# A pooled attention with a top-2 mixture of experts: whole-row gathers and scatters, spread over partition groups through scratch, late zeros and a moved drain

## The chip, the core and the metric

The kernel runs on one core of one Trainium2 chip. The metric is the device time of one execution in microseconds; lower is better. The core has five engines: PE (TensorE) multiplies matrices, DVE (VectorE) and ACT (ScalarE) work elementwise, POOL (GpSimd) works elementwise and issues the indirect DMAs, that is gathers and scatters whose row numbers come from a tile, and SP (SyncE) issues plain DMAs. Each engine carries out its instructions in order and waits for others by semaphores.

## The reference

Two parts follow each other. The attention has 8 batches, 8 heads, 576 tokens, head size 64; keys and values are first averaged over groups of 8 tokens, so each query meets 72 pooled rows. Its output, 4608 tokens of 512 numbers, goes through a noisy top-2 mixture of 8 experts (512 to 1024 to 512):

```python
k_p = k.reshape(B, H, Sp, pool, D).mean(axis=3)
v_p = v.reshape(B, H, Sp, pool, D).mean(axis=3)
attn = softmax(scale * np.matmul(q, k_p.transpose(0, 1, 3, 2)))
x = (attn @ v_p).transpose(0, 2, 1, 3).reshape(4608, 512)
noisy = x @ w_gate + np.log1p(np.exp(x @ w_noise)) * noise
# the two largest of 8 per token; their softmax weighs the two experts
for e in range(E):
    for k in range(2):
        mask = top2[:, k] == e
        h = np.maximum(x[mask] @ w1[e], 0.0)
        out[mask] += top2_w[mask, k, None] * (h @ w2[e])
```

(The softmax is written out in the reference; it is shortened here.) Each token is thus worked on by two experts, and its two contributions are added in its row of the output.

## The kernel before

**Attention.** Work goes in 4 pairs of batches, each cut into 9 chunks of 128 tokens, 36 chunks in all. Eight of the nine (kind "D") belong to one batch; the ninth (kind "R") holds the last 64 tokens of both. SP loads q, k and v. Keys and values are pooled by adding halves: the first addition of the values of batches 2 to 7 is on POOL (`halves`, L237, chosen by the bit mask PV = 252), the others on DVE (L243, L249). `pe_prep` multiplies the pooled values by a mask into block tiles `vbd` on POOL (L317, main part) and DVE (L332). `qk` (L371, L378) makes scores, `et` transposes their exponentials, `av` (L410) multiplies by `vbd`. A row multiply on DVE (L421) makes the chunk's x, kept as `lastx`, which SP or POOL writes to `x_dram` (L428, L431).

**Zeros.** The output is added to row by row, so it is first filled with zeros: `zero` (L124) is nine plain DMAs of 1 MB on SP, one in each of the chunks from 27 on. They stand under `issue_after(lastx[0].ins)`, which orders them in the program and makes SP wait for nothing.

**Routing.** `route` finds each token's two experts and weights and its place in each expert's list. For each 128 tokens and each of the two choices, POOL scatters 128 records of 8 bytes (token number, weight) into `rec_dram` (L593, 72 DMAs). `load_recs` (L621) reads the lists back and works out the index tiles. For expert 0 these hold token numbers. For the others `late()` and `spread()` work out, by small matmuls with a selection matrix (L634), a quarter-row index: each row of x is seen as four rows of 128 numbers, and each 32 tokens of a tile are spread so that every partition group of 32 holds a quarter of their row (`x4`, `out4`, `oi4`, `wc4`).

**Experts.** The list of an expert is cut into tiles of 128 tokens. Three groups follow each other: tiles 0 to 3, then the tail (tiles 7 to 9, at most 320 tokens, of which PE picks one of three widths, 320, 272 or 240, by the count), then tiles 4 to 6. For group i the program emits in this order: `stage1` of group i (first product, L943, by 8 blocks of 128 hidden units; ACT takes the ReLU into `hh`, L950; DVE takes the rest into `hl`, L951), `split` of group i+1, `fetch` of group i+2, `stage2` of group i. Every product is done in three passes of high and low parts in fp32r. The framework orders the instructions of each engine by priority and readiness.

`fetch` gathers rows of x on POOL. For expert 0 it is one indirect DMA per tile (L675). For the others it is four per tile (two for tile 9), each of 128 quarter rows (L683):

```python
for r in range(2 if t == 9 else 4):
    nc.gpsimd.indirect_dma_start(
        out=xg[:, r * P:(r + 1) * P], out_offset=None, in_=x4,
        in_offset=bass.IndirectOffsetOnAxis(ap=xi[e, t][:, r], axis=0))
```

There are four buffers `xg`. `split` transposes a tile, on PE for expert 0 (L871), else on DVE by 32 x 32 blocks (L877), and makes the high part on ACT and the low part on DVE (L882).

`stage2` of a group of full tiles takes each tile by itself: `prev` reads the present rows of the output (L963, one whole-row gather on POOL into one of three `pv` buffers), 24 matmuls (L1037), `finish` adds the weighted result on DVE in four parts (L978), and POOL scatters the rows back (L981). A first `prev` of an expert has to wait for the last scatter of the expert before. The tail's `stage2` makes the transposed product (L1008), transposes it back on DVE by 32 x 32 blocks into `yt` (L1015), and works by quarter rows: 10 gathers of the output (L995), 10 additions on DVE (L1021), 10 scatters (L1024).

**Weights.** `weights` loads 512 KB pieces on SP (L458, 64 of them) into three staging buffers `wst`; ACT makes the high part (L468) and DVE the low (L469).

After the last group comes a loop for tokens beyond the lists' capacity, which makes no trip with these inputs, and a closing barrier with drains of each engine (L1215).

## Time and profile before

| | |
|---|---|
| time, median of 3 runs | 1265.1 us (1261.36 to 1266.04) |
| profiled execution | 1265.68 us |
| its span in the profile | 1263.9 us |
| mean granted clock of TensorE | 0.903 |
| PE busy | 1082.7 us (86%), 5858 matmuls |
| DVE / ACT busy | 559.8 us (44%) / 343.7 us (27%) |
| POOL busy | 687.2 us (54%), 690 instructions |
| first matmul of the experts | at 263.0 us |
| last matmul | ends at 1248.1 us |

The span is what the profiler saw of one execution; the execution's time is 1.8 us longer. A granted clock of 1.00 is 2.4 GHz and 0.50 is 1.2 GHz; a mean between them is a mixture of both. "issue" as the releaser of an idle time means that the engine waited for nothing that the profile shows. Times in the rows are microseconds from the start of the span.

### The profile page before, as it was taken

The numbers are of one execution on the slowest core, as the hardware profiler recorded it, in microseconds if no ns is written. First come the engines' busy times: TensorE is split into PE (matmuls) and PEld (weight loads), VectorE is DVE, ScalarE is ACT, GpSimd is POOL, SyncE is SP. The second block draws the span as 40 slices with busy tenths as digits, with TensorE's granted clock in tenths as the row PEclk, the third lists the DMA queues.
The fourth block names the chain that finished last, engine by engine and source line by source line (L and its number), as shares of the span: only waits on it lengthen the run. The fifth ranks groups of instructions, "written<-read, shape, count | busy, mean of one in ns | idle before, by whom it ended". The sixth has DMA issues, their size and how long they took to land. (4 is left out here: it accounts for less than half of the span.)

```text
span 1263.9 us, 16358 instructions
## 1 busy us (share of the span) xinstructions
PE 1082.7 (86%) x5858; PEld 937.6 (74%) x5858; DVE 559.8 (44%) x1323; ACT 343.7 (27%) x862; POOL 687.2 (54%) x690
## 2 busy tenths in 40 slices
PE   7887698369899878979997899899989997898895
PEld 6876588258788578858885788588869885786794
DVE  5786557363236233614361436234513551361341
ACT  4675376140123012301230123013301330131110
POOL 3345553726547635773577357645764576566131
PEclk7999689679899788989898889799979998999897
DMA  9998795233115221522152215221622261222110
GB/s 265 311 303 175 188 283 189 56 117 86 44 42 176 69 67 51 188 69 62 51 175 76 63 52 184 66 72 51 196 56 71 50 196 53 74 52 74 52 32 27
DMA packets 78143, 141.05 MB, mean 112 GB/s; under 512 B 26391, under 2 KB 34604, under 8 KB 78036
## 3 DMA queue, kind: packets, MB, share of 16 engines
q1 hardware_dynamic: 49876, 76.88, 21.3%
q0 software_dynamic: 28160, 62.70, 16.9%
q8 instruction: 73, 1.20, 0.4%
q14 instruction: 34, 0.28, 0.1%
HBM read 102.27 MB, written 39.17 MB: 112 GB/s over the span
## 5 line engine op out<-in xcount | busy, mean ns | idle before, releaser
L943 PE MATMUL ph<-xh,w 128*128 128x384 f32 (+4 forms) x1536 | 417.6, 352 | 59.6 <-ACT xh L882 25.3
L683 POOL DMA_INDIRECT xg<-x_dram,x x266 | 283.5, 1066 | 143.6 <-issue 74.4
L943 PEld LDWEIGHTS ph<-xh,w 128*128 128x128 f32 x1536 | 286.9, 199 | 91.6 <-issue 35.6
L1037 PE MATMUL py<-w,hh 128*128 128x512 f32 x896 | 300.2, 412 | 25.1 <-issue 22.8
L943 PE MATMUL ph<-xl,w 128*128 128x512 f32 (+4 forms) x768 | 270.1, 352 | 4.2 <-issue 3.2
L950 ACT ACTIVATE hh<-ph 128x512 fp32r<-128x512 f32 (+2 forms) x192 | 97.0, 508 | 638.8 <-PE ph L943 204.2
L1037 PEld LDWEIGHTS py<-w,hh 128*128 128x128 f32 x896 | 176.7, 199 | 73.7 <-issue 39.0
L951 DVE SCALAR_TENSOR_TENSOR hl<-ph,hh 128x512 fp32r<-128x512 f32 (+2 forms) x192 | 109.2, 577 | 255.9 <-ACT hh L950 196.2
L1037 PE MATMUL py<-w,hl 128*128 128x512 f32 x448 | 185.2, 413 | 15.8 <-issue 15.3
L943 PEld LDWEIGHTS ph<-xl,w 128*128 128x128 f32 x768 | 152.5, 199 | 19.6 <-issue 5.8
L978 DVE SCALAR_TENSOR_TENSOR pv<-py,raw,pv 128x128 f32<-128x128 f32 x196 | 54.8, 343 | 242.2 <-remote 142.8
L1024 POOL DMA_INDIRECT out_dram<-pv,o x80 | 82.9, 1036 | 80.2 <-DVE pv L1021 53.0
L981 POOL DMA_INDIRECT out_dram<-pv,raw x56 | 57.5, 1027 | 123.6 <-DVE pv L978 108.3
L1037 PEld LDWEIGHTS py<-w,hl 128*128 128x128 f32 x448 | 88.8, 198 | 43.5 <-issue 26.5
L593 POOL DMA_INDIRECT rec_dram<-rec,pos x72 | 73.2, 1016 | 75.7 <-DVE cum L1122 23.8
L1008 PE MATMUL py<-hh,w 128*128 128x240 f32 (+2 forms) x512 | 99.8, 293 | 0.1
L469 DVE TENSOR_TENSOR w<-wst,w 128x512 fp32r<-128x512 f32 x128 | 82.9, 685 | 22.7 <-issue 9.6
L468 ACT CAST w<-wst 128x512 fp32r<-128x512 f32 x128 | 73.0, 618 | 70.3 <-DMA wst<-in_moe_w_dram 50.7
L1008 PEld LDWEIGHTS py<-hh,w 128*128 128x128 f32 x512 | 82.5, 192 | 0.8 <-issue 0.8
L995 POOL DMA_INDIRECT pv<-out_dram,o x70 | 71.4, 1020 | 21.3 <-issue 19.2
L385 ACT ACTIVATE ex<-s,mx 128x72 f32<-128x72 f32 x288 | 69.2, 340 | 30.9 <-DVE mx L383 29.9
L1008 PE MATMUL py<-hl,w 128*128 128x240 f32 (+2 forms) x256 | 74.9, 292 | 1.3 <-issue 1.3
(153 smaller groups left out, 1063.9 us busy)
## 6 DMA issues: line engine op xcount, KB each, us to landing
wst<-in_moe_w_dram SPq DMA_DIRECT2D x64, 512.0 KB
v<-in_v_dram SPq DMA_DIRECT2D x24, 448.0 KB
out_dram<-zt SPq DMA_DIRECT2D x9, 1024.0 KB
k<-in_k_dram SPq DMA_DIRECT2D x7, 1280.0 KB
q<-in_q_dram SPq DMA_DIRECT2D x7, 1024.0 KB
x_dram<-xr POOLq DMA_DIRECT2D x12, 512.0 KB
xg<-x_dram,x POOLq DMA_INDIRECT x276
x_dram<-xr SPq DMA_DIRECT2D x4, 512.0 KB
```

The costliest lines, as they stand in the source:

```text
L385: nc.scalar.activation(ex[:, jj, EPOS[h] * G:(EPOS[h] + 1) * G], sv[:, i], AF.Exp, bias=mx[:, i:i + 1])
L468: nc.scalar.copy(hv, sv)
L469: nc.vector.tensor_sub(lv, sv, hv.bitcast(F32))
L593: s = nc.gpsimd.indirect_dma_start(out=rec_dram[:, :], out_offset=bass.IndirectOffsetOnAxis(ap=pos[:, i, c:c + 1], axis=0), in_=rec[:, c, ...
L683: nc.gpsimd.indirect_dma_start(out=xg[:, r * P:(r + 1) * P], out_offset=None, in_=x4, in_offset=bass.IndirectOffsetOnAxis(ap=xi[e, t][:, r ...
L943: nc.tensor.matmul(part(ph), w1s(e, a, db, f), part(xs[b][:, db]), start=(i == 0), stop=(i == 3 * NDB - 1))
L950: nc.scalar.activation(hh[:, :n], ph[:, :n], AF.Relu)
L951: nc.vector.scalar_tensor_tensor(hl[:, :n], ph[:, :n], 0.0, hh[:, :n].bitcast(F32), op0=OP.max, op1=OP.subtract)
L995: g = nc.gpsimd.indirect_dma_start(out=pv4[:, i], out_offset=None, in_=out4, in_offset=bass.IndirectOffsetOnAxis(ap=oi4[e, t0 + i // 4][:, ...
L1008: nc.tensor.matmul(part(py), w2s(e, b, f)[:, mb * P:(mb + 1) * P], part(hs[f][a]), start=(i == 0), stop=(i == 3 * NFB - 1))
L1024: s = nc.gpsimd.indirect_dma_start(out=out4, out_offset=bass.IndirectOffsetOnAxis(ap=oi4[e, t0 + i // 4][:, i % 4], axis=0), in_=r4[:, i], ...
L1037: nc.tensor.matmul(py, hs[f][a][:, cs], w2s(e, b, f), start=(i == 0), stop=(i == 3 * NFB - 1))
```

## The change

- The quarter-row indices are taken out: `sel`, `qcol`, `late`, `spread` with its small matmuls, `oi4`, `wc4`, `x4`, `out4`, `pv4`. The index tile is worked out directly from the records, on POOL for expert 0 and on DVE for the others.
- `gather` of experts 1 to 7 becomes one whole-row indirect DMA per tile into `row` (two buffers), a plain DMA by SP of that tile into a DRAM scratch `via` (four buffers), and four plain DMAs by SP (two for tile 9) from there into the four quarters of `xg`.
- The tail reads the output by `prev`, whole rows of three tiles, so that it uses the three `pv` buffers too. Its transposed result goes from `yt` by ten plain DMAs of SP into a scratch `viay`, by three more into `ys`, and each of its three tiles is finished by one wide DVE instruction and one whole-row scatter.
- `zero` gets a real dependency: each of the nine DMAs waits for the row multiply (DVE) of its chunk.
- PV becomes 0: the values' halves are added on DVE. The main part of `vbd` (16 products) goes from POOL to DVE.
- In chunks of kind R, the scores of both row halves are emitted together, alternating, and the loops of `av` alternate the two token halves.
- In the last `stage1`, after its fourth block, POOL drains, ordered after the last scatter sent by then.

```diff
-    PK, PV = 0, 252
+    PK, PV = 0, 0
@@
-            nc.gpsimd.tensor_mul(vb[:BST, ss, :D].rearrange("p (n i) d -> p n i d", i=ns),
+            nc.vector.tensor_mul(vb[:BST, ss, :D].rearrange("p (n i) d -> p n i d", i=ns),
@@
+            if g == 0:
+                SR[u] = [ps2.tile([P, 512], F32, tag="s", name=f"s{nm}_{k}", bufs=SB) for k in range(2)]
+                for i in range(4):
+                    for b2 in range(2):
+                        for k in range(2):
+                            nc.tensor.matmul(SR[u][k][b2 * 64:b2 * 64 + 64, i * G:(i + 1) * G],
...
@@
-            for r in range(2 if t == 9 else 4):
-                nc.gpsimd.indirect_dma_start(
-                    out=xg[:, r * P:(r + 1) * P], out_offset=None, in_=x4,
-                    in_offset=bass.IndirectOffsetOnAxis(ap=xi[e, t][:, r], axis=0))
+            nr = 2 if t == 9 else 4
+            row = pools[0].tile([P, DM], F32, tag="row", name=f"row{e}_{t}", bufs=2)
+            nc.gpsimd.indirect_dma_start(
+                out=row[:32 * nr], out_offset=None, in_=x_dram[:, :],
+                in_offset=bass.IndirectOffsetOnAxis(ap=xi[e, t][:32 * nr], axis=0))
+            via = dp.tile([P, DM], F32, tag="via", name=f"via{e}_{t}", bufs=4)
+            nc.sync.dma_start(via[:32 * nr], row[:32 * nr])
+            for r in range(nr):
+                nc.sync.dma_start(xg[:, r * P:(r + 1) * P],
+                                  via[32 * r:32 * r + 32].rearrange("j (u c) -> u j c", u=4))
@@
-                with tc.issue_after(lastx[0].ins):
-                    zero((i - ZS) // ZD)
+                zd = zero((i - ZS) // ZD)
+                tc.add_manual_dep(zd.ins, lastx[0].ins.name,
+                                  mybir.DependencyInfo(mybir.DependencyClass.Sync, mybir.DependencyReason.DATA),
+                                  reason="paced by the chunks")
@@
+            pvs = [prev(e, t, P) for t in range(7, 10)]
...
+            for t in range(7, 10):
+                nr = 2 if t == 9 else 4
+                ys = mp.tile([P, DM], F32, tag="ys", name=f"ys{e}_{t}", bufs=2)
+                via = dp.tile([P, DM], F32, tag="viay", name=f"viay{e}_{t}", bufs=3)
+                for r in range(nr):
+                    nc.sync.dma_start(via[32 * r:32 * r + 32].rearrange("j (u c) -> u j c", u=4),
+                                      yt[:, 4 * (t - 7) + r].rearrange("p m c -> p (m c)"))
+                nc.sync.dma_start(ys[:32 * nr], via[:32 * nr])
+                finish(e, t, P, ys, pvs[t - 7], 32 * nr)
             return
@@
+    def flush(f):
+        if f == 3:
+            with tc.issue_after(sent[-1].ins):
+                nc.gpsimd.drain()
@@
-        stage1(g, (hook0, hook2)[i] if i < 2 else None)
+        stage1(g, hook0 if i == 0 else flush if i == len(groups) - 1 else None)
```

## Rows read from the trace of the kernel before

**Rows 1.** Busy time in stretches, one for each expert (experts 2 and 6 here, the longest and the shortest of experts 1 to 6). Columns: stretch, its length, busy time (and instructions) of PE, weight loads, DVE, ACT and POOL, mean granted clock, mean DMA share, GB/s.

```profile
515.20:642.30 127.10, 115.22 (x554) 99.04 (x553) 51.37 (x104) 27.12 (x52) 75.80 (x72) 0.92 0.31 92
...
1015.90:1136.50 120.60, 107.53 (x554) 91.50 (x553) 49.86 (x101) 24.75 (x48) 76.45 (x74) 0.94 0.28 84
```

**Rows 2.** The same view for the matmuls of one line alone, in stretches in which that line runs without a pause: the first product with 512 columns (L943), the second with 512 (L1037), the first with 384 (L943), the tail's second with 320 (L1008). Columns: stretch, length, busy PE (and matmuls), clock, DMA share, GB/s.

```profile
642.20:664.30 22.10, 21.92 (x96) 1.00 0.60 194
1231.60:1248.20 16.60, 16.52 (x72) 1.00 0.10 35
1216.30:1231.80 15.50, 15.44 (x88) 1.00 0.09 28
589.30:600.20 10.90, 10.72 (x72) 1.00 0.16 43
```

**Rows 3.** Stretches inside expert 2, columns as in rows 1.

```profile
556.00:571.30 15.30, 7.71 (x18) 3.92 (x17) 0.33 (x2) 0.00 (x0) 8.92 (x10) 0.67 0.23 69
571.30:605.90 34.60, 32.89 (x196) 31.11 (x195) 13.00 (x29) 5.15 (x11) 15.85 (x17) 0.95 0.21 65
605.90:611.20 5.30, 3.36 (x12) 2.21 (x11) 0.33 (x1) 0.49 (x1) 1.72 (x2) 0.79 0.14 37
611.20:642.30 31.10, 31.10 (x147) 28.25 (x146) 21.15 (x45) 11.02 (x21) 19.05 (x15) 0.93 0.30 82
```

**Rows 4.** The timeline of the weight loads between 556 and 571 us, two following ones. Columns: start, duration, engine, line, operation, count; in brackets the idle time before and its releaser.

```profile
556.89 0.19 PEld L1037 LDWEIGHTS py<-w,hh 128*128 128x128 f32 x1 [0.51 <-issue]
557.57 0.19 PEld L1037 LDWEIGHTS py<-w,hl 128*128 128x128 f32 x1 [0.50 <-issue]
```

**Rows 5.** The timeline of POOL in expert 2: the first and the last of the run of 27 indirect DMAs (3 of L963, 10 of L995, 8 of L683, one each of L981 and L963, 4 of L683), and the first and the last of the run of twelve of L683.

```profile
532.62 1.04 POOL L963 DMA_INDIRECT pv<-out_dram,raw  x1 [2.01 <-DMA out_dram<-pv,raw]
...
566.71 0.95 POOL L683 DMA_INDIRECT xg<-x_dram,x  x1 [0.30 <-issue]
...
593.13 0.98 POOL L683 DMA_INDIRECT xg<-x_dram,x  x1 [5.26 <-DVE xt L877]
...
606.98 0.95 POOL L683 DMA_INDIRECT xg<-x_dram,x  x1 [0.30 <-issue]
```

**Rows 6.** The same slow stretches in experts 1 and 3 to 6 (a short one of expert 1 stands second), columns as in rows 1.

```profile
423.00:438.00 15.00, 9.54 (x21) 4.68 (x20) 1.13 (x4) 0.00 (x0) 9.34 (x10) 0.67 0.15 38
479.50:486.00 6.50, 3.31 (x11) 2.27 (x10) 0.00 (x0) 0.06 (x1) 3.16 (x4) 0.74 0.15 42
681.00:699.30 18.30, 9.17 (x18) 4.13 (x16) 1.12 (x4) 0.00 (x0) 11.60 (x12) 0.58 0.24 68
802.50:815.70 13.20, 8.10 (x17) 3.48 (x15) 0.00 (x0) 0.00 (x0) 7.92 (x9) 0.67 0.17 42
926.40:939.00 12.60, 7.23 (x16) 3.88 (x16) 0.00 (x0) 0.00 (x0) 7.65 (x8) 0.63 0.16 42
1045.60:1063.30 17.70, 10.43 (x34) 5.92 (x33) 0.00 (x0) 0.00 (x0) 11.62 (x12) 0.89 0.15 39
```

**Rows 7.** Expert 0: the first and the last of a run of twelve on POOL's timeline, and the busy times of the stretch around it, columns as in rows 1.

```profile
315.52 0.97 POOL L683 DMA_INDIRECT xg<-x_dram,x  x1 [0.99 <-issue]
...
329.36 0.95 POOL L683 DMA_INDIRECT xg<-x_dram,x  x1 [0.30 <-issue]
...
315.50:333.00 17.50, 12.75 (x80) 12.37 (x79) 2.92 (x7) 1.70 (x5) 11.44 (x12) 0.79 0.20 56
```

**Rows 8.** PE's waits between 388.8 and 1248 us: the one for the split's copy by ACT, which lies in expert 7. Columns: engine and line, what was waited for, us in total, times, longest.

```profile
PE ph L943 <- ACT xh L882: 8.3, 1, 8.3
```

**Rows 9.** SP. Its waits over the whole span (for the copy that frees a staging buffer of weights, and for the plain write of a table that it reads back next), and the issue of the weight loads and of the zeros: duration of one in ns (least, median, most), first and last start.

```profile
SPq L458 <- DVE w L469: 359.3, 33, 103.7
...
SPq L1143 <- DMA tab_dram<-tab: 2.8, 1, 2.8
...
L458 SPq DMA_DIRECT2D wst<-in_moe_w_dram x64: 327/368/5317, 159.1 to 1121.3; - x64
...
L124 SPq DMA_DIRECT2D out_dram<-zt x9: 540/1607/3565, 121.9 to 180.4; - x9
```

**Rows 10.** POOL's waits between 388.8 and 1248 us: the first read of the output in an expert, for the scatter before it to land.

```profile
POOL pv L963 <- DMA out_dram<-pv,raw: 14.0, 7, 2.0
```

**Rows 11.** Groups of instructions by line and shape in the attention: the values' halves and the mask products on POOL, an addition of 1536 columns on DVE, a mask product of 160 columns on DVE; and one addition on DVE's timeline with its wait. Columns: count, busy us, mean ns of one, idle before and releaser.

```profile
L237 POOL TENSOR_TENSOR v<-v 112x768 f32<-112x768 f32 x12 | 21.6, 1812 | 5.8 <-DMA v<-in_v_dram 5.7
...
L317 POOL TENSOR_TENSOR vbd<-vs,vmask 112x512 f32<-112x512 f32 x8 | 8.5, 1064 | 16.6 <-PE a L410 9.0 <-DVE vs L249 7.5
L317 POOL TENSOR_TENSOR vbd<-vs,vmask 112x128 f32<-112x128 f32 x8 | 5.1, 637 | 0.0
...
L243 DVE TENSOR_TENSOR v<-v 112x1536 f32<-112x1536 f32 x2 | 3.5, 1754 | 1.6 <-DMA v<-in_v_dram 1.6
...
L332 DVE TENSOR_TENSOR vbd<-vr,vmask 112x160 f32<-112x160 f32 x8 | 2.6, 323 | 2.9 <-PE vr L330 1.7 <-remote 1.2
...
139.13 5.65 DVE L243 TENSOR_TENSOR v<-v 112x768 f32<-112x768 f32 x1 [10.66 <-POOL v L237]
```

**Rows 12.** The step from the attention to the experts: the first of 28 record scatters that follow each other on POOL's timeline, and the busy times of the stretch before the first product, columns as in rows 1.

```profile
222.99 1.00 POOL L593 DMA_INDIRECT rec_dram<-rec,pos  x1 [15.15 <-DVE rt L513]
...
235.00:263.00 28.00, 3.59 (x15) 2.39 (x13) 4.27 (x13) 3.92 (x8) 20.47 (x23) 0.50 0.20 37
```

**Rows 13.** The end: the last scatter on POOL's timeline, and the drains of POOL (ns: least, median, most).

```profile
1249.58 0.97 POOL L981 DMA_INDIRECT out_dram<-pv,raw  x1 [4.47 <-DVEq L1149]
...
L1215 POOLq DRAIN  x3: 46/103/8815, 1254.2 to 1263.6; - x3
```

More of the change, by code (lines that the diff above doesn't have):

```diff
@@ L89 @@
             nc.vector.scalar_tensor_tensor(col, prow, float(hi), col, op0=OP.is_lt, op1=OP.mult)
-    sel = cp.tile([P, 4, 4, 32], F32, name="sel")
-    nc.gpsimd.tensor_copy(sel, ident.rearrange("p (r j) -> p r j", j=32).unsqueeze(2).to_broadcast([P, 4, 4, 32]))
-    qcol = cp.tile([P, 1], F32, name="qcol")
-    for i in range(4):
-        nc.gpsimd.memset(qcol[32 * i:32 * i + 32], float(i))
     before = cp.tile([P, P], BF16, name="before")
@@ L123, in zero @@
         zt = zts[0]
[L124 to L125 removed]
+        return nc.sync.dma_start(out[i * ZW * P:(i + 1) * ZW * P, :].rearrange("(p r) m -> p r m", p=P),
+                                 zt.unsqueeze(1).to_broadcast([P, ZW, DM]))
     ZW = 4
@@ L365, in qk @@
                 return
-            rows = []
-            for i in range(4):
-                h = 2 * i + g
-                rows.append((0, h))
-                for b2 in range(2):
-                    nc.tensor.matmul(s[b2 * 64:b2 * 64 + 64, i * G:(i + 1) * G],
-                                     qT[g * 64:g * 64 + 64, i, b2 * 64:b2 * 64 + 64],
-                                     kbd[b2][g * 64:g * 64 + 64, h, g * G:(g + 1) * G],
-                                     start=True, stop=True)
+            if g == 0:
[4 more added lines that the diff above has]
+                            nc.tensor.matmul(SR[u][k][b2 * 64:b2 * 64 + 64, i * G:(i + 1) * G],
+                                             qT[k * 64:k * 64 + 64, i, b2 * 64:b2 * 64 + 64],
+                                             kbd[b2][k * 64:k * 64 + 64, 2 * i + k, k * G:(k + 1) * G],
+                                             start=True, stop=True)
+            s = SR[u][g]
+            rows = [(0, 2 * i + g) for i in range(4)]
         else:
+            s = ps2.tile([P, 512], F32, tag="s", name=f"s{nm}", bufs=SB)
             rows = [(jj, h) for h in GRP[g] for jj in range(2)]
@@ L404, in av @@
         halves = ((slice(0, P), b),) if kind == "D" else ((slice(0, 64), b), (slice(64, P), b + 1))
-        for ts_, bb in halves:
-            vb = vbd[bb % 2]
-            for n in range(NEB):
-                hs, half = HEADS[n], HEADS[n][0] // 4
-                blocks = [m for m in range(NEB) if HEADS[m][0] // 4 == half]
+        for n in range(NEB):
+            hs, half = HEADS[n], HEADS[n][0] // 4
+            blocks = [m for m in range(NEB) if HEADS[m][0] // 4 == half]
+            for ts_, bb in halves:
+                vb = vbd[bb % 2]
                 nc.tensor.matmul(
@@ L662, in load_recs @@
                 i = (e - e0, t - t0)
-                xi[e, t] = x[:, i[0], i[1]:i[1] + 1] if e == 0 else x[:, :, i[0], i[1]:i[1] + 1]
+                xi[e, t] = x[:, i[0], i[1]:i[1] + 1]
                 tokc[e, t] = raw[:, i[0], i[1], 0:1]
                 wcol[e, t] = raw.bitcast(F32)[:, i[0], i[1], 1:2]
-        return late
     XG = {}
-    out4 = out.rearrange("n (u c) -> (n u) c", u=4)
-    x4 = x_dram.rearrange("n (u c) -> (n u) c", u=4)
     def gather(e, t):
@@ L898 @@
         pvb.append(t)
-    pv4 = mp.tile([P, 10, P], F32, name="pv4")
-    nc.gpsimd.memset(pv4, 0.0)
     rows = {}
@@ L992, in stage2 @@
             yt = mp.tile([P, 10, NDB, 32], F32, tag="yt", name=f"yt{e}")
-            if e:
-                for i in range(10):
-                    g = nc.gpsimd.indirect_dma_start(
-                        out=pv4[:, i], out_offset=None, in_=out4,
-                        in_offset=bass.IndirectOffsetOnAxis(ap=oi4[e, t0 + i // 4][:, i % 4], axis=0),
-                        bounds_check=4 * NTOK - 1, oob_is_err=False)
-                    tc.declare_no_dep(g.ins, group=f"out{e}", reason="rows of other tokens")
-                    tc.add_to_no_dep_group(f"out{e}", g.ins)
+            pvs = [prev(e, t, P) for t in range(7, 10)]
             for mb in range(NDB):
@@ L1015, in stage2 @@
                 nc.vector.transpose(yt[:, :, mb], py[:, :n].rearrange("p (c j) -> p c j", j=32))
-            r4 = pv4
-            for i in range(10):
-                y = yt[:, i].rearrange("p m j -> p (m j)")
-                wc = wc4[e, t0 + i // 4][:, i % 4]
-                if e:
-                    nc.vector.scalar_tensor_tensor(r4[:, i], y, wc, pv4[:, i], op0=OP.mult, op1=OP.add)
-                else:
-                    nc.vector.tensor_scalar(r4[:, i], y, wc, None, op0=OP.mult)
-                s = nc.gpsimd.indirect_dma_start(
-                    out=out4, out_offset=bass.IndirectOffsetOnAxis(ap=oi4[e, t0 + i // 4][:, i % 4], axis=0),
-                    in_=r4[:, i], in_offset=None, bounds_check=4 * NTOK - 1, oob_is_err=False)
-                tc.declare_no_dep(s.ins, group=f"out{e}", reason="rows of other tokens")
-                tc.add_to_no_dep_group(f"out{e}", s.ins)
+            for t in range(7, 10):
[7 more added lines that the diff above has]
+                finish(e, t, P, ys, pvs[t - 7], 32 * nr)
             return
```

65 lines of the change are left out of this document (19 added, 46 removed).

## The prediction

> **What bounds the kernel now.** I began with the stretches of the eight experts [rows 1]. The reader is to see that experts 1 to 6 last 120 to 127 us although PE is busy for only some 91% of that, at a mean granted clock near 0.9. Next I worked out what an expert would last if PE never paused. Windows in which one kind of matmul stands alone give the pace [rows 2]: 96 matmuls of 512 columns take 21.92 us (0.228 each), 72 second-product matmuls of 512 take 16.52, 88 of 384 take 15.44 (0.175 each), 72 of 320 take 10.72 (0.149 each). Expert 2 needs 96 and 96 of 512, 96 and 96 of 320 in its tail, 96 of 384 and 72 of 512: 21.9 + 22.0 + 14.3 + 14.3 + 16.8 + 16.5 = 105.8 us. It took 127.1, so 21.3 us are lost inside one expert.
>
> Cutting expert 2 into five stretches shows where [rows 3]. From 556.0 to 571.3 only 18 matmuls ran, in 15.3 us, at clock 0.67, which is a mixture of the 1.2 and 2.4 GHz levels. From 605.9 to 611.2 twelve ran, at 0.79. The weight loads of the first stretch come one per 0.7 us, and the idle time before each is "issue": PE waits for no semaphore that the trace shows [rows 4]. No data is late there; the instructions themselves come slowly. So I asked what the other engines do just then. POOL issues indirect DMAs without a break from 532.62 to 566.71, at a pitch of 1.3 us, and the second stretch lies at the end of a run of twelve from 593.13 to 606.98 [rows 5]. The same pairing stands in all of experts 1 to 6: a long stretch of 12.6 to 18.3 us in each, and a short one [rows 6]. That pairing, not a wait, is what I take as the bound: a long unbroken run of POOL's indirect DMAs starves PE of instructions. It isn't proven. In expert 0 a run of twelve, 315.52 to 329.36, goes with a window in which PE still gets through 80 matmuls in 17.5 us, at clock 0.79 [rows 7]. Length alone doesn't fix the size of the loss.
>
> **The change, part by part.** The sum is made against the profiled execution's 1265.7 us, 0.6 us above the median shown of 1265.1.
>
> *Gathers, tail reads and tail scatters as whole rows.* For experts 1 to 7, four quarter-row gathers per tile become one (38 of them per expert become 10), ten quarter reads of the tail become three, ten quarter scatters become three. The unbroken run of 27 [rows 5] becomes one of 3 + 3 + 3 + 2 = 11 at most, if nothing holds any of them back, and of six or seven where the waits between groups stay; the run of twelve becomes one of three. What the runs cost now: the long stretches of experts 1 to 6 are 15.0 + 15.3 + 18.3 + 13.2 + 12.6 + 17.7 = 92.1 us, with 21 + 18 + 18 + 17 + 16 + 34 = 124 matmuls, worth 124 x 0.228 = 28.3 us at pace; lost 63.8. The short ones lose 5.3 - 12 x 0.175 = 3.2 us in expert 2 and 6.5 - 11 x 0.175 = 4.6 in expert 1 [rows 3, 6]; at 4 each, 24. Behind them the clock is still low: 34.6 us at 0.95 and 31.1 at 0.93 give back 1.7 + 2.2 = 3.9 us per expert, 23 for six. I take all three as gone: -111 us (bounds 0 and -128, which is 6 x 21.3, everything that an expert like expert 2 loses). Expert 7 has one idle time of 8.3 us in front of its tail's first matmul, for a split that came late, behind a run of thirteen [rows 8]: -8 (0 to -9). In expert 0 the window [rows 7] has 4.8 us without a matmul and loses 0.21 x 17.5 = 3.7 at the lower clock, 8.5 in all; its gathers for expert 1 make two runs, and I take half of twice that: -8 (0 to -17).
>
> *The detour through scratch.* Each tile of an expert's gather now passes one indirect DMA, a write to DRAM by SP, and four reads by SP; each tail tile four writes, one read, one addition, one scatter. The nearest row to a hop is SP's wait for its own plain write of a small table before reading it back, 2.8 us; SP's issue takes 0.33 to 0.37 us [rows 9]. For a gathered tile: 1.3 + about 2.0 (landing, as the wait of the first tail read for a scatter [rows 10]) + 0.4 + 2.8 + 4 x 0.4 + 2.8 = 10.9 us, and three more tiles follow at 1.3 to 2.0 us each, so some 16 us for a group. The four input buffers come free when one group is split and are needed when the next is, one stage or more (22 us and up, [rows 2]) later. Hidden, with 6 us or more to spare. For the tail: 4 x 0.4 + 2.8 + 0.4 + 2.8 + 0.6 + 1.3 + 2.0 us until the first of three shared result buffers is free, and 3.3 more until the next group's earlier output rows are in it: 14.8 us, against 16.8 of first products and 5.5 (24 matmuls of 512) of the first second product. Hidden, but by 7 us only, and each later tile needs its own. I take 2 us per expert as showing, for seven: +14 (bounds 0 and +178, the last rival). The ten small additions of the tail become three wide ones; DVE isn't the limit there, so nothing.
>
> The Trainium skill, "DMA: Bandwidth & Descriptors", section "Anatomy of one DMA", puts a fixed cost of about 2.0 us on a transfer, mostly completion; the two hops would be 4.0 us by it, an estimate, where the row of 2.8 gives 5.6. The measured row is the dearer, and the sum above goes by the row.
>
> *Off POOL, on to VectorE.* POOL loses 12 additions (21.6 us) and 16 mask products (13.6); VectorE gets 6 more additions of 1.75 us and 16 products of 0.3 to 0.7 (128 and 512 columns, by a 160-column product of 0.32 and an addition of 1536 columns of 1.75, scaled by columns): some 10.5 + 8 = 18.5 us [rows 11]. What speaks for it: at 139.13 VectorE had waited 10.7 us for POOL's half, which stood behind nine scatters. Against it: VectorE is the fullest engine of the attention. Bounds: -25 (that wait and as much again of PE's stop) to +18.5 (all of the new work exposed). I take the wait won, 10.7, less a seventh of the new work, 2.7: -8. The alternated row halves of the last 64 tokens save at most a part of 40-odd small matmuls; nothing, bounded in the same range.
>
> *Late zeros.* Nine transfers of 1 MB, which SP now starts from 121.9 on [rows 9], wait for chunks 27 to 35. In front of them nothing is gained by PE; behind each on SP stand the first expert's weights. The end of the attention isn't the start of the MoE: from 235 to 263 us PE gets 15 matmuls through, behind a run of 28 record scatters that begins at 222.99 [rows 12], which the change keeps. So zero, 0 to +10.
>
> *One drain.* After the last scatter, at 1249.58, nothing runs for 13.3 us, and 8.8 of it is POOL's drain [rows 13]. A drain in the last first-product stage takes what was queued by then, under 15.4 us of matmuls. Three scatters and three reads still come after. -6 (0 to -8.8).
>
> Sum: -111 - 8 - 8 + 14 - 8 + 0 - 6 = -127, so 1265.7 - 127 = 1138.7, about **1139 us**.
>
> **Rivals.** A, the forecast, 1139, with its own range of 1085 (all 128 us won, attention at its lower bound) to 1175.
>
> B: the runs are broken, but SP, which works in order, holds the scratch transfers up behind weight loads that wait for a free staging buffer. SP stood so 33 times for 359.3 us, 10.9 on average, longest 103.7 [rows 9]. If one such mean wait per expert shows beyond what I counted, 8.9 x 7 = 62 us return: 1201. For it: 48 plain transfers more per expert for the gathers and 13 for the tail, all on SP. Against it: the weight loads of an expert are eight in 120 us, so SP is mostly free.
>
> C: PE's slow stretches don't come from the number of indirect DMAs, but from something that stays (the bytes in 512-byte pieces, or the code that PE must fetch for the tail's three variants). Rows 7 speak for it: a run of twelve with a mild loss. Against it: the long stretch comes in all six experts at the end of the longest run. Then attention and drain alone remain: 1265.7 - 8 - 6 = 1252.
>
> D, slower: SP's order decides. Where SP waits for a tile's scratch write to land before its read, everything behind it, weights too, stands; and the tail's scatter, POOL's next, holds up the gathers behind it. Two mean waits of 10.9 and two hops of 2.8 in the open are 27.4 us per expert, 25.4 beyond the 2 counted, 178 for seven: 1139 + 178 = 1317. It decides from 18 us per expert (127 / 7) upward. Against it stand the 6 and 7 us of cover and that both chains lie beside matmuls.
>
> For D speaks a rule of the Trainium skill, same page, section "Two DMAs through the same engine are not ordered": the issuing engine has to wait on the first transfer's semaphore before it issues the one that depends on it. SP's 2.8 us row is that wait in this trace, so the trace agrees.
>
> **Chances.** A 0.53, B 0.25, C 0.12, D 0.10. A measurement of this kernel tells a change of about 0.5% from none, some 6.3 us. Faster: A, B and 0.09 of C, 0.87; same: 0.03 of C and 0.01 of D, 0.04; slower: 0.09. The time is A's, 1139. The range goes from 1085 to 1225, which holds A and the better part of B; C and D lie outside, 2 in 10.
>
> **What would show it.** Right: experts 1 to 6 at 100 to 110 us, granted clock near 1.0 in them, no stretch with "issue" before weight loads; VectorE's wait for POOL in the attention gone; POOL's last drain under 3 us. B shows as PE waiting for a split or for VectorE's copy of a result, with SP waiting for weights ahead of it. C shows as the same slow stretches beside POOL runs of six. I am wrong if the experts stay above 115 us, whichever wait is named then.

## The result and the profile after

The changed kernel took 1176.5 us (median of four, 1175.95 to 1178.36) where the kernel before took 1265.2 in the same set: ratio 0.931, 95% interval 0.929 to 0.933. The forecast was 1139, the range 1085 to 1225. The profiled execution took 1175.95 us, its span 1174.1, against 1263.9 before: 89.8 us less, where the sum had 127.

One fact is needed for all that follows: the kernel before, unchanged, took 1265 to 1284 us in three sets of runs and 1094 to 1099 in two others, and one chip, chip 11, gave it both ways. In the first condition PE's instructions come slowly beside POOL's runs, in the second they don't (experiments 1, 3 and 4). I call them "slow issue" and "no slow issue". The result above and the profile before belong to slow issue. Ratios below are always to the kernel before in the same set.

The page of the kernel after, its first two parts:

```profile
PE 1027.4 (88%) x5826; PEld 905.4 (77%) x5826; DVE 551.7 (47%) x1285; ACT 343.6 (29%) x862; POOL 352.0 (30%) x351
...
POOL 2004461725314333522433413120312031213203
PEclk8999988679699899799979999999999999999999
```

POOL does half of what it did (690 instructions before, 351 now), and in the second half of the span the clock is nearly full. The same stretches as in [rows 1], one line per expert from 1 to 7:

```profile
377.60:499.30 121.70, 106.61 (x553) 92.09 (x552) 52.20 (x101) 26.03 (x50) 49.03 (x45) 0.92 0.61 194
499.30:626.40 127.10, 111.76 (x553) 97.08 (x552) 50.04 (x95) 26.03 (x50) 44.35 (x43) 0.93 0.61 190
626.40:736.80 110.40, 103.20 (x554) 91.06 (x554) 47.18 (x90) 26.03 (x50) 31.05 (x28) 0.98 0.52 164
736.80:849.10 112.30, 107.17 (x554) 95.05 (x553) 50.38 (x96) 26.03 (x50) 23.74 (x20) 0.98 0.37 115
849.10:961.10 112.00, 107.22 (x554) 95.28 (x553) 48.56 (x94) 26.02 (x50) 23.85 (x20) 0.98 0.36 112
961.10:1067.00 105.90, 100.34 (x553) 88.57 (x552) 51.23 (x98) 25.94 (x50) 24.07 (x20) 0.98 0.37 119
1067.00:1167.30 100.30, 98.61 (x553) 87.53 (x551) 34.61 (x76) 15.31 (x30) 22.13 (x21) 1.00 0.22 68
```

Experts 6 and 7 are within the forecast 100 to 110 us, experts 3 to 5 just above it (110.4 to 112.3). Experts 1 and 2 are nearly or quite as slow as before (126.4 and 127.1 us), with a DMA share of 0.61 instead of 0.31. PE's waits over the whole span say what took over (engine and line, what was waited for, us in total, times, longest):

```profile
PE ph L913 <- DVE hl L921: 40.8, 18, 6.5
PE xp L843 <- issue: 21.9, 3, 8.6
PE py L1001 <- DVE hl L921: 20.9, 7, 8.3
```

"issue" is gone from both products (it had stood in front of the weight loads of [rows 4]). What is left of it, 21.9 us, stands before the transposes of expert 0's first split, between 212.6 and 237.6 us, beside an unbroken run of 28 record scatters on POOL (206.0 to 241.5 us) that the change kept; the same transposes had 13.4 us of it in the kernel before, and 1.1 in experiment 1, without slow issue. In the products PE waits for something else now. It waits for `hl`, the low part of the hidden values, from VectorE. VectorE's timeline in expert 1 shows why (start, duration, engine, line, what; idle time before and its releaser), and PE's and SP's stand beside it:

```profile
463.12 0.56 DVE L921 SCALAR_TENSOR_TENSOR hl<-ph,hh 128x384 fp32r<-128x384 f32 x1 [1.52 <-ACT hh L920]
478.89 0.75 DVE L952 SCALAR_TENSOR_TENSOR pv<-ys,raw,pv 128x512 f32<-128x512 f32 x1 [15.22 <-DMA ys<-viay]
479.56 0.55 DVE L921 SCALAR_TENSOR_TENSOR hl<-ph,hh 128x384 fp32r<-128x384 f32 x1
```

```profile
480.17 0.80 PE L1001 MATMUL py<-w,hl 128*128 128x512 f32 x1 [7.54 <-DVE hl L921]
```

```profile
441.76 14.71 SPq L652 DMA_DIRECT2D via<-row  x5
456.57 9.23 SPq L654 DMA_DIRECT2D xg<-via  x12
465.90 1.08 SPq L652 DMA_DIRECT2D via<-row  x2
467.08 6.07 SPq L989 DMA_DIRECT2D viay<-yt  x8
474.33 0.33 SPq L991 DMA_DIRECT2D ys<-viay  x1
```

The tail's last transpose into `yt` ended at 457.9. SP was then in the middle of gather transfers, for tiles that VectorE took up from 486 us on and for later ones, and began the tail's writes at 467.08. The tail's first addition became ready at 478.9. It stands in VectorE's queue in front of the `hl` that PE needs, so VectorE stood still for 15.2 us and PE for 7.5, and PE's clock fell (granted 1.00 before the stop, 0.50 from 480 to 491 us): the 72 matmuls of that second product took 30.9 us instead of 16.5, and those of expert 2 about as long.

The gathers run ahead because nothing holds them. By 467 us SP had issued 34 of the 70 row writes to scratch while VectorE had taken up 12 tiles, so the four buffers asked for `via` were no bound; the last was issued at 681.6, when expert 3 was being worked on, while the reads go on to 1071.4. From expert 3 on the tail's transfers are no longer late, and the second products of the third group take 16.4 us.

```profile
L652 SPq DMA_DIRECT2D via<-row x70: 319/322/2089, 294.2 to 681.6; - x70
...
L654 SPq DMA_DIRECT2D xg<-via x266: 507/598/4625, 310.1 to 1071.4; - x133
```

One loss stays in all of experts 1 to 6: their first product with 512 columns takes 26.5 to 28.8 us, where [rows 2] has 21.9. There `hl` stands on VectorE behind a low part of weights, which waits for ACT's high part, and this for a weight load; in expert 4 (PE waits 2.8 us for the `hl` that follows):

```profile
749.31 1.29 DVE L465 TENSOR_TENSOR w<-wst,w 128x512 fp32r<-128x512 f32 x2 [3.92 <-ACT w L464]
```

The end: POOL's drains (ns: least, median, most), where [rows 13] had 8815, and the drain that was moved:

```profile
L1178 POOLq DRAIN  x3: 46/103/382, 1172.9 to 1173.8; - x3
```

```profile
L1045 POOLq DRAIN  x1: 4952/4952/4952, 1154.8 to 1154.8; - x1
```

From the last matmul to the end of the span it is 6.9 us now, 15.8 before.

### The profile page after: what moved, and what is told of

The parts are those of the page before. It is cut to its first block, busy times and chain, and to the rows that moved or that the text cites. A ratio compares the mean times of both kernels' runs of the same rounds, so it can differ in the third digit from the quotient of the medians.

```text
span 1174.1 us, 16356 instructions
## 1 busy us (share of the span) xinstructions
PE 1027.4 (88%) x5826; PEld 905.4 (77%) x5826; DVE 551.7 (47%) x1285; ACT 343.6 (29%) x862; POOL 352.0 (30%) x351
## 3 DMA queue, kind: packets, MB, share of 16 engines
q1 hardware_dynamic: 108124, 122.24, 34.8%
q0 software_dynamic: 23824, 62.67, 17.4%
## 5 line engine op out<-in xcount | busy, mean ns | idle before, releaser
L913 PE MATMUL ph<-xh,w 128*128 128x384 f32 (+4 forms) x1536 | 411.3, 348 | 49.4 <-DVE hl L921 40.8
L913 PEld LDWEIGHTS ph<-xh,w 128*128 128x128 f32 x1536 | 280.9, 195 | 81.4 <-DVE hl L921 40.3
L1001 PE MATMUL py<-w,hh 128*128 128x512 f32 x896 | 283.6, 397 | 0.0
L913 PE MATMUL ph<-xl,w 128*128 128x512 f32 (+4 forms) x768 | 266.6, 347 | 1.1 <-DVE xl L854 1.1
L955 POOL DMA_INDIRECT out_dram<-pv,raw x80 | 99.6, 1246 | 398.5 <-DVE pv L952 370.1
L1001 PEld LDWEIGHTS py<-w,hh 128*128 128x128 f32 x896 | 171.7, 193 | 34.4
L1001 PE MATMUL py<-w,hl 128*128 128x512 f32 x448 | 179.6, 401 | 20.9 <-DVE hl L921 20.9
L648 POOL DMA_INDIRECT row<-x_dram,x x70 | 70.1, 1001 | 168.4 <-DMA via<-row 157.3
L933 POOL DMA_INDIRECT pv<-out_dram,raw x70 | 77.0, 1100 | 64.8 <-issue 33.0
L849 DVE STREAM_TRANSPOSE xt<-xg 128x512 f32<-128x512 f32 (+1 forms) x70 | 70.8, 1032 | 21.4 <-DMA xg<-via 21.0
```

Of the source, the lines that this page charges most:

```text
L648: nc.gpsimd.indirect_dma_start(out=row[:32 * nr], out_offset=None, in_=x_dram[:, :], in_offset=bass.IndirectOffsetOnAxis(ap=xi[e, t][:32 * ...
L849: nc.vector.transpose(xt[:, :nr], xg[:, :nr * P].rearrange("p (r i b) -> p r b i", i=32, b=NDB))
L913: nc.tensor.matmul(part(ph), w1s(e, a, db, f), part(xs[b][:, db]), start=(i == 0), stop=(i == 3 * NDB - 1))
L933: g = nc.gpsimd.indirect_dma_start(out=pv[:np_], out_offset=None, in_=out, in_offset=bass.IndirectOffsetOnAxis(ap=tokc[e, t][:np_], axis=0 ...
L955: s = nc.gpsimd.indirect_dma_start(out=out, out_offset=bass.IndirectOffsetOnAxis(ap=tokc[e, t][:np_], axis=0), in_=res[:np_], in_offset=No ...
L1001: nc.tensor.matmul(py, hs[f][a][:, cs], w2s(e, b, f), start=(i == 0), stop=(i == 3 * NFB - 1))
```

## The experiments

**1. The tail alone** (kernel before, with the new tail: `prev` of three tiles, scratch, wide additions).

```diff
-            if e:
-                for i in range(10):
-                    g = nc.gpsimd.indirect_dma_start(
-                        out=pv4[:, i], out_offset=None, in_=out4,
...
+            pvs = [prev(e, t, P) for t in range(7, 10)]
```

> The kernel before with the tail part of the change alone: three whole-row reads and scatters for the tail instead of ten and ten, its result through scratch; gathers in quarter rows, attention, zeros and end as before. Run theory (a long unbroken run of POOL's indirect DMAs starves PE of instructions): the run of 27 is 20 now, so the long stretch with 'issue' shrinks to about 6 us but stays, and the short one beside the twelve gathers stays whole; experts 1 to 6 at about 118, in all 1205 to 1235 us. Rival (the slow stretches come from something that the change left in place, and the gain of the experts is of another kind): the long stretch stays at 12 us or more, 1250 to 1275. Head-of-line theory (VectorE's wide addition waits for the scratch transfers in front of work that PE needs): with SP free of gather transfers, that addition is ready early, VectorE waits under 6 us for it, and PE's waits for hl stay under 15 us in all.

1105.7 us, ratio 1.011 (1.006 to 1.015): this set had no slow issue, which none of the theories had foreseen. Its POOL runs are long (23 indirect DMAs without a break here, one per 1.5 us), and PE doesn't mind. First and last of a run, and the busy times of that stretch and of experts 1 and 2:

```profile
438.84 1.00 POOL L982 DMA_INDIRECT out_dram<-pv,raw  x1 [8.85 <-DVE pv L979]
...
472.63 1.01 POOL L982 DMA_INDIRECT out_dram<-pv,raw  x1 [0.30 <-issue]
```

```profile
438.80:473.60 34.80, 33.87 (x150) 27.67 (x149) 25.13 (x46) 14.06 (x26) 28.05 (x23) 1.00 0.67 208
354.60:455.40 100.80, 98.71 (x554) 87.59 (x553) 49.62 (x95) 25.74 (x50) 61.13 (x58) 1.00 0.41 126
455.40:564.00 108.60, 105.69 (x554) 94.23 (x553) 50.18 (x97) 26.77 (x52) 62.62 (x59) 1.00 0.40 121
```

34.8 us of POOL without a pause, and PE is busy for 33.9 of them at full clock. So a long run alone doesn't slow PE: the condition must be there too. VectorE waited 36.7 us in all for the tail's scratch, 3.8 at most: with SP free of gathers the tail's detour costs about 1%, some 12 us. PE's waits for `hl` came to 20.9 us, where under 15 was expected.

**2. The old tail** (kernel after, with the ten quarter reads, additions and scatters of before, and one `row` buffer instead of two).

```diff
-            pvs = [prev(e, t, P) for t in range(7, 10)]
+            if e:
+                for i in range(10):
+                    g = nc.gpsimd.indirect_dma_start(
+                        out=pv4[:, i], out_offset=None, in_=out4,
...
-            row = pools[0].tile([P, DM], F32, tag="row", name=f"row{e}_{t}", bufs=2)
+            row = pools[0].tile([P, DM], F32, tag="row", name=f"row{e}_{t}", bufs=1)
```

> The kernel after with the tail of the kernel before: ten quarter reads, ten small additions, ten quarter scatters, no scratch for the tail (and one buffer for gathered rows instead of two, for room). Run theory: runs of thirteen reads come back, with gathers behind them under twenty; a stretch with 'issue' of 3 to 8 us per expert comes back. Head-of-line theory: the 30 us second products of the third group in experts 1 and 2 fall back to 17, since no addition waits for scratch; together 1165 to 1195 us. If the scratch detour of the tail were free, the time would be 1195 or more.

1207.6 us, ratio 1.104 (1.097 to 1.112), same set, above the expected 1165 to 1195. The long second products are back at 16.5 us as expected, but the first products of the first group take 30 to 47 us in experts 1 to 6. The waits of PE, of ACT and of SP:

```profile
PE ph L949 <- DVE hl L957: 128.3, 21, 22.1
...
ACT w L469 <- DMA wst<-in_moe_w_dram: 222.9, 31, 22.1
...
SPq L685 <- DMA row<-x_dram,x: 430.6, 53, 24.5
```

SP waits for a row gather to land before it may write it to scratch, weight loads stand behind it, ACT waits for weights, VectorE's low parts of weights for ACT, and `hl` behind these. One buffer less made the wait longer than in the kernel after, so the 128 us isn't the kernel after's price; the path is the same one.

**3 and 4. Idle gathers** (kernel after, with 26 quarter-row gathers that nothing reads, in each of experts 1 to 7), once in each condition.

```diff
+            if e:
+                for i in range(26):
+                    nc.gpsimd.indirect_dma_start(
+                        out=junk[:, i % 6], out_offset=None, in_=x4,
+                        in_offset=bass.IndirectOffsetOnAxis(ap=xi[e, 4], axis=0))
```

> The kernel after with 26 quarter-row gathers into an unused tile behind the tail's three reads in experts 1 to 7, so that POOL again has a run of about 29 indirect DMAs there; nothing reads them. Run theory: a stretch of 10 us or more with weight loads at one per 0.7 us and 'issue' in front of them comes back in every one of the seven experts, granted clock falls to 0.9 or under in them, 1250 to 1310 us (the gathers also hold POOL for 34 us). Rival (the slow stretches came from what the gathers and scatters were for, not from their number): no such stretch; PE loses only where a scatter behind the run is late, 1176 to 1215 us with the idle times put down to DVE or ACT.

With no slow issue: 1269.6 us, ratio 1.160 (1.155 to 1.166). The time lies in the range of the run theory, but that is luck, for its mechanism didn't act. The idle gathers ran ahead into experts 0 to 2. PE's "issue" came to under 3 us in all; PE lost by VectorE, which stood up to 45.6 us before an addition whose read was queued behind the idle gathers:

```profile
PE ph L913 <- DVE hl L921: 117.7, 19, 40.6
...
PE xp L843 <- issue: 1.6, 2, 1.2
```

```profile
DVE pv L955 <- DMA pv<-out_dram,raw: 67.8, 5, 45.6
```

> The kernel after with the 26 idle gathers once more, since the first time it met the condition without slow issue (1270 us, no 'issue' before weight loads, VectorE waiting up to 45 us for reads queued behind the idle gathers). Run theory: where the kernel before takes about 1270, the idle runs bring back weight loads at one per 0.7 us with 'issue' in front of them in each of experts 1 to 7, 30 us or more of such idle time in all, and the time is 1290 or more. Rival (slow issue belongs to what the gathers are for): no more 'issue' on PE than the kernel after has, about 1275.

With slow issue: 1387.7 us (one execution). The same 182 idle gathers, and now PE's first waits, one stretch, and its weight loads there:

```profile
PE ph L913 <- issue: 101.3, 30, 21.2
PE ph L913 <- DVE hl L921: 75.7, 20, 22.6
PE py L984 <- issue: 40.3, 22, 3.1
PE xp L843 <- issue: 39.5, 7, 14.8
```

```profile
618.50:669.10 50.60, 9.88 (x28) 7.02 (x28) 1.62 (x3) 0.00 (x0) 33.00 (x35) 0.53 0.31 95
```

```profile
626.06 0.29 PEld L984 LDWEIGHTS py<-hh,w 128*128 128x128 f32 x1 [1.18 <-issue]
628.41 0.29 PEld L984 LDWEIGHTS py<-hl,w 128*128 128x128 f32 x1 [2.06 <-issue]
```

28 matmuls in 50.6 us. Transfers that nothing waits for brought the slow issue back: it goes with POOL's indirect DMAs and not with what they are for. It didn't come "in each of experts 1 to 7": the idle gathers all stood in experts 0 to 2, the last at 713.6 us, and from 730 us on PE shows no "issue", as the run theory has it for where they really stood. These gathers bring back the number and the 512-byte pieces together, so they don't tell the two apart; the record scatters, which have pieces of 8 bytes and 21.9 us of "issue" beside them in the kernel after, speak for the number.

**5. Late additions** (kernel after, tail additions emitted behind the next first product's last block, three result buffers `ys` instead of two).

```diff
-                finish(e, t, P, ys, pvs[t - 7], 32 * nr)
+                pend.append(lambda t=t, ys=ys, nr=nr: finish(e, t, P, ys, pvs[t - 7], 32 * nr))
```

> The kernel after with the tail's three wide additions and scatters emitted behind the last block of the next group's first product (and three buffers for the result instead of two). Head-of-line theory: VectorE no longer waits for scratch in front of hl; the second products of the third group in experts 1 and 2 fall from 31 us to 17, 25 to 30 us are won, 1145 to 1155 us. Rival (PE waits there because of SP, which is late with weights as well, or of DMA load of the gathers that run ahead): under 8 us are won, and another wait stands in the same place, 1168 to 1180 us.

1162.9 us, ratio 1.064 (1.059 to 1.069), no slow issue. A miss: the framework orders VectorE's queue by its own reckoning and put the additions in front of `hl` again (at 461.87 VectorE had waited 14.67 us for scratch; second products of the third group still 28.6 and 30.9 us in experts 1 and 2). So this is nearly the kernel after in the condition without slow issue: some 6% slower than the kernel before. The kernel after itself wasn't met in that condition.

**6 to 8. Both kernels again, and all but the experts.** The kernel after and the kernel before unchanged, and the kernel after with the gathers and tail of before, which leaves values and mask products on VectorE, alternating halves, late zeros and the drain.

> The kernel after, unchanged, because the kernel before took 1094 us on the chip of the first four experiments and not 1265. Chip theory (PE's slow issue beside POOL's long runs belongs to some chips, the cost of the scratch detour to all): where the kernel before takes about 1094, the kernel after takes 1150 to 1180 and is slower than it by 5 to 8%; where it takes about 1265, the kernel after takes about 1177. Rival (the chip of the first four was quicker in everything): the kernel after would be quicker there by as much, 1000 to 1040.

> The kernel before, unchanged, for its trace on this chip. Chip theory: at about 1094 us the same long runs of indirect DMAs stand on POOL, at the same pitch of 1.3 us, and PE shows no weight loads with 'issue' in front of them; experts 1 to 6 take 100 to 110 us. At about 1265 us the trace is that of the first profile.

> The kernel after with the gathers and the tail of the kernel before: what is left of the change is the values and mask products on VectorE, the alternating halves, the late zeros and the drain. If these are worth what the end of the attention and the end of the span showed in the first pair of profiles (16.5 and 8.9 us), the time is 20 to 28 us under that of the kernel before on the same chip, whichever chip it is: about 1068 to 1074 beside 1094, or 1238 to 1245 beside 1265. If the attention's gain also came from PE's slow issue, only 8 to 12 us are left where there is none of it.

This set had slow issue, on the chip that had shown none in the experiments so far: the condition isn't the chip's alone. After 1179.6 (0.922, 0.917 to 0.928); before 1274.5 in its profile; the third 1254.6 (0.981, 0.977 to 0.986), 24.3 us less than the median of the kernel before, as expected. Its trace has "issue" in front of both products as the kernel before has (here the third, then the kernel before again), so it is the whole rows of gathers and tail that end it:

```profile
PE py L1046 <- issue: 37.3, 45, 2.2
PE ph L946 <- issue: 27.2, 43, 1.6
```

```profile
PE ph L943 <- issue: 29.2, 37, 2.0
PE py L1037 <- issue: 27.8, 34, 1.5
```

**9. Two holds** (kernel after; each row gather waits for the split of the tile eight tiles earlier, the tail's additions are ordered behind the last `hl`, and there are three buffers `ys`).

```diff
+            if gone[0] > 8:
+                tc.add_manual_dep(g.ins, xts[gone[0] - 8 - 1].ins.name,
+                                  mybir.DependencyInfo(mybir.DependencyClass.Sync, mybir.DependencyReason.DATA),
+                                  reason="paced by the splits")
...
+                with tc.issue_after(low.ins):
+                    while pend:
+                        pend.pop(0)()
```

> The kernel after with two holds on the detour: each row gather of experts 1 to 7 waits for the split of the tile eight tiles earlier, so that gathers don't run ahead through the scratch, and the tail's additions are ordered behind the last hl of the next first product. Head-of-line theory: SP is free for the tail's transfers when its result is there, VectorE's additions no longer stand in front of hl, the second products of 29 to 31 us fall to 17; 25 to 45 us under the kernel after on the same chip. Rival (it is the sheer number of transfers on SP): under 10 us.

1149.0 us, ratio 0.899 (0.894 to 0.903), 30.6 under the kernel after in the same set, as expected: what stood in front in a queue was the cause of that part. The two holds were only tried together, so what each gives isn't told apart. All second products of the third group take 16.5 us, and VectorE's wait for scratch fell from 64.7 us (kernel after, same set) to this:

```profile
DVE pv L965 <- DMA ys<-viay: 5.2, 6, 1.8
```

```profile
PE ph L922 <- DVE hl L930: 43.2, 14, 6.5
```

What stays is `hl` in the first product of experts 1 to 6 (27 to 29 us instead of 21.9), behind late weights, as in the kernel after. It beats both kernels in this condition.

**10 and 11. Weights from ACT** (the two holds, with weight loads of experts 1 to 7 issued by ACT), beside the kernel after.

```diff
-            nc.sync.dma_start(dst, src)
+            (nc.scalar if e else nc.sync).dma_start(dst, src)
```

> The kernel with the two holds (row gathers paced by the splits, the tail's additions behind the last hl) and, in addition, the weight loads of experts 1 to 7 issued by ACT instead of SP. Head-of-line theory for the weights: with the holds, what is left of PE's waits is hl in the first product of experts 1 to 6 (27 to 29 us instead of 22), because VectorE's low parts of weights stand in front of hl and wait for ACT's high parts, these for weight loads that stand on SP behind transfers waiting for an input buffer. Loads on ACT bring the first products to 23 us or less; 25 to 36 us less than the kernel with the two holds, which was 30 under the kernel after: 1112 to 1125 beside an after of 1177. Rival (ACT, waiting for a free staging buffer, now holds back its own ReLU): first products unchanged or longer, 1145 or more, with PE's waits for ACT's hh.

> The kernel after once more beside these. Theory of two conditions (the same chip gives the kernel before 1094 us in one set of runs and 1279 in another, by whether PE's issue is slow beside POOL's runs): with the kernel before at about 1270 it takes 1175 to 1185; with the kernel before at about 1094 it takes 1160 to 1180, since the scratch detour costs the same in both and only 'issue' in front of expert 0's transposes (some 20 us) goes.

1161.1 us, ratio 0.907 (0.899 to 0.915), beside 1174.2 for the kernel after (0.916, 0.909 to 0.923; 1175 to 1185 was expected). A miss: 13 us under the kernel after instead of 50 and more. The wait for `hl` was longer and not shorter, and the first products of experts 1 to 6 took 27 to 33 us. VectorE's wait for earlier output rows is there too, as long as with the two holds alone (25.1 us):

```profile
PE ph L922 <- DVE hl L930: 53.4, 17, 7.3
```

```profile
DVE pv L965 <- DMA pv<-out_dram,raw: 24.7, 9, 6.5
```

ACT as the issuing engine doesn't bring the weights earlier (it waited 110.4 us for them in all, 117.4 with the two holds alone). So SP's order isn't shown to be why they are late; what is remains open.

**12. Old gathers, new tail** (kernel after with the quarter-row gathers of before).

```diff
-            nc.gpsimd.indirect_dma_start(
-                out=row[:32 * nr], out_offset=None, in_=x_dram[:, :],
...
+            for r in range(2 if t == 9 else 4):
+                nc.gpsimd.indirect_dma_start(
+                    out=xg[:, r * P:(r + 1) * P], out_offset=None, in_=x4,
```

> The kernel after with the quarter-row gathers of the kernel before and the new tail: no scratch for gathers, scratch for the tail. On a chip in the condition without slow issue (kernel before about 1094): the tail alone cost 1.0% there (1106), and the attention and the drain were worth 24 us in the other condition; 1075 to 1092, quicker than the kernel before and far quicker than the kernel after would be. In the condition with slow issue (kernel before about 1275): the ten quarter reads and ten quarter scatters per expert are gone and 38 quarter gathers stay; run theory: runs of twelve and sixteen remain, so half of the 'issue' in front of PE's weight loads remains, 1160 to 1210; VectorE's waits for scratch under 15 us, first products of 22 to 24 us. Rival (only the gathers count): PE's 'issue' in the experts as large as in the kernel before, 1230 or more.

On chip 12, no slow issue: 1092.8 us beside 1099.3, ratio 0.995 (0.992 to 0.997), just above the expected 1075 to 1092. Experts 1 and 2 of its profile:

```profile
346.10:447.60 101.50, 98.76 (x554) 87.67 (x553) 49.88 (x96) 26.18 (x51) 61.80 (x58) 1.00 0.41 126
447.60:558.90 111.30, 107.21 (x554) 95.33 (x553) 51.30 (x98) 27.18 (x52) 62.77 (x59) 0.98 0.40 118
```

Without the gathers' detour the experts run nearly at pace; where there is no slow issue this is the better kernel, by half a per cent over the kernel before, and the gathers' change is worth less than nothing. With slow issue it wasn't tried.

## Why the prediction was right, and where it was wrong

From the end of expert 0's last matmul to the end of expert 7's the profiles give, with slow issue, 859.2 us (before), 789.4 (after) and 761.4 (two holds); with none, 791.3 (late additions, nearly the kernel after) and 734.8 (old gathers, new tail). Two things are read from these five. With the detour the experts last the same in both conditions (the other two profiles of the kernel after, with slow issue, gave 796.2 and 787.9), so as far as single profiles tell, the change removed slow issue from experts 1 to 7. And 789 - 735 = some 55 us is what the gathers' detour costs; it was compared directly without slow issue alone (791 against 735).

The tail's detour stands in four of the five figures. By experiment 1 it costs some 12 us, so slow issue and the whole detour are each larger than the differences below by about that, an estimate across sets.

- *Whole rows, -111 and -8 for expert 7.* Right in kind and nearly in size: 859.2 - 734.8 = 124 us of slow issue, some 136 with the tail's share, against 119. My doubt by [rows 7], that length alone doesn't fix the loss, was justified further than I knew: it hangs on a condition that one profile can't show.
- *The detour, +14.* This is the step that failed: "I take 2 us per expert as showing". It cost 55 for the gathers, some 67 with the tail. I worked out when the data would be there and set that against the time of the matmuls, as though SP and VectorE had nothing else in their queues. About half of the 55, 28 us, lies in the third group's second products of experts 1 and 2 (61.2 us together, 32.8 in experiment 12): in front of the tail's writes stood gather transfers that SP issues far ahead, and behind the waiting addition on VectorE stood `hl`. I had asked who is behind a waiting instruction on SP and POOL, and not on VectorE. The other half, 26 us, lies in the first products of experts 1 to 6 (166.0 us together, 140.1 in experiment 12), where `hl` stands behind late weights; why these are late is open. By the sign that I had set (above 115 us) I was wrong for experts 1 and 2.
- *Expert 0, -8.* It got 5.4 us longer (125.9 to 131.3). Six row gathers of the next expert stand on POOL in front of the last two of its own, and PE waits there 6.4 us for a gather and 6.5 for `hl`.
- *Off POOL, -8.* The first product starts 16.5 us earlier (246.5 against 263.0); VectorE's 10.7 us wait for POOL is gone. I had called VectorE the fullest engine of the attention; PE is fuller (139.2 us busy of the 175 from 60 to 235 us in the kernel before, VectorE 120.5). In single profiles, expert 1 starts 17.1 us earlier in experiment 8 than in the kernel before of its set, with slow issue, and 8.5 us earlier in experiment 12 than in experiment 1, without it and of different sets. In that second pair the first product itself starts 26.2 us earlier, and expert 0 then lasts 17.7 us longer, with one wait of 17.4 for `hl`. How much of the 16.5 was relief of slow issue isn't shown. The zeros were not tried alone.
- *One drain, -6.* It gave 8.9 (15.8 to 6.9), all that stood in the way. It is the moved drain and not POOL's fewer instructions: in experiment 8, with the old gathers and scatters, it took 16.6 us beside matmuls and the last drain 0.3, while experiment 1, which has no moved drain, ends with one of 8.9.

Together: -69.8 + 5.4 - 16.5 - 8.9 = -89.8 us, the difference of the spans. That the last three terms miss by amounts that nearly cancel (13.4 against 8.5 and 2.9) is luck, and so is that the result was taken with slow issue: without it, by the nearest relative of the kernel after, the change would have come out slower.

Of the rivals, A holds for the issue, though 1176.5 lies just above its own range of 1085 to 1175. B holds in kind for what came back, with another order than it named: gather transfers in front, not weight loads. Priced at 62 us beyond the 14, it turned out 41 for the gathers, some 53 with the tail. C is refuted by the profile after: the code for the tail's widths stays, and so do the 512-byte pieces, on SP, while the "issue" before the products is gone; the idle gathers brought it back. D's 18 us per expert were not reached (8, or nearly 10 with the tail). For D I had named a rule of the Trainium skill, "DMA: Bandwidth & Descriptors", section "Two DMAs through the same engine are not ordered"; the trace agrees, SP waited 32 times and 29.6 us in all for its own writes of the tail to land before reading them back. Beside that it waited 39 times and 147.1 us for a row gather to land before writing it on.

## What to carry to other kernels

When a step gets a longer chain of transfers, look at each engine of the chain for what is queued behind the instruction that waits, VectorE and ACT too, and for transfers without a hold that run ahead and stand in front; a chain that fits beside the matmuls can still stop them. An unexplained "issue" before matmuls is worth pairing with what other engines do just then, but take the pair of kernels in more than one set of runs before building on it: here one change is 7% faster in one condition and, by its nearest relative, 6% slower in the other.

## What the runs showed of the hardware

Not expected: one kernel on one chip took 1094 us in one set and 1279 in another, each set being even within 1.5%. With the condition, 28 matmuls passed in 50.6 us beside POOL's indirect DMAs, one per 1.25 us; without it, PE was busy 33.9 of 34.8 us beside a run of one per 1.5 us, and beside the same idle gathers it had under 3 us of "issue" in all. What sets the condition is open: it isn't the chip alone, since chip 11 had both, and no run here varied anything that could tell.

POOL's closing drain took 8.8 to 8.9 us in the kernels without an earlier drain, in either condition, and 0.3 to 0.8 in those with one. The earlier drain took 4.5 to 16.6 us, beside matmuls; what sets its length isn't shown.
